# A small load of two rows of x per DMA engine, issued ahead of c, at the start of a DiT block

## The chip, the cores and the metric

The kernel runs on one core of one Trainium2 chip. The metric is the device time of one execution in microseconds (us). Executions quoted here: 3 to 11 of each kernel in one set of rounds; a span or a start time comes from the one profiled execution of that kernel. PE is the matmul engine, PEld its weight load, DVE the vector engine, ACT the scalar engine, POOL GpSimd; SPq and ACTq are the queues from which DMAs are issued.

## The reference, cut to what matters

```python
B, N, D = (2, 256, 1152)
mod = (_silu(c) @ w_mod).reshape(B, 6, 1, D)
shift_a, scale_a, gate_a, shift_m, scale_m, gate_m = [mod[:, i] for i in range(6)]
h = _layernorm(x, axis=-1) * (1 + scale_a) + shift_a
qkv = (h @ wqkv).reshape(B, N, 3, H, Dh)
# ... attention, output projection, second layernorm, two large matmuls with gelu
return x + gate_m * m
```

Only the first line of work matters here: the layernorm of x and the scale that comes from c. They must be done before the first large matmul can run.

## The kernel before

x is loaded as four tiles of 128 tokens, in the order 0, 1, 3, 2 (0 and 1 are batch 0). c goes out on the scalar queue at the same moment. Behind x come the weights; the first of them is w_scale_a, the columns of w_mod that make scale_a.

```python
    x_sb = act.tile([P, NT, D], BF16, name="x_sb", tag="x_sb")
    c_sb = act.tile([B * KD, P], BF16, name="c_sb")
    nc.scalar.dma_start(c_sb[:], c_v)
    for t in (0, 1, 3, 2):
        nc.sync.dma_start(x_sb[:, t, :], x_v[:, t // TPB, t % TPB, :])
    # ... constants, then the weights on the sync queue behind x
```

PE warms up on zeros, transposes c, and goes on warming up. ACT and DVE make `sT`, silu of c transposed:

```python
    warm(2, pwarm)
    nc.tensor.transpose(pc[:], c_sb[:], ident[0:B * KD, 0:B * KD])
    nc.scalar.activation(sig[:], pc[:], ACT.Exp, scale=-1.0)
    nc.vector.tensor_scalar_add(sig[:], sig[:], 1.0)
    nc.vector.reciprocal(sig[:], sig[:])
    nc.vector.tensor_tensor(sT..., pc..., sig..., op=ALU.mult)   # arguments cut
```

The layernorm statistics are divided: ACT takes tiles 0 and 2 (two passes each, into `sink`), DVE takes tiles 1 and 3.

## Time and profile before

| | before |
|---|---|
| time | 243.78 us median of 3 (243.64 to 244.18) |
| span of the profiled execution | 241.8 us |
| PE busy | 235.4 us, 97% |
| PE starts tile 2's transposes | 11.41 us |
| from there to the start of the last stage (at 168.34 us, in the chain of waits) | 156.93 us |

From the profile page of the kernel before: busy time by engine, the granted clock of PE in 40 slices (in tenths), and the chain of waits by engine.

```profile
PE 235.4 (97%) x1688; PEld 144.4 (60%) x1698; DVE 91.5 (38%) x193; ACT 59.9 (25%) x121; POOL 28.3 (12%) x47
...
PEclk9999999999999999999999999999999999999999
...
PE 94%; issue 2%; ACT 2%; POOL 1%; DVE 0%; POOLq 0%; DVEq 0%; ACTq 0%
```

The reader sees a kernel bound by PE from end to end. In this trace, a change at the start can only save or cost time where PE still waits, which is before 11.4 us. The next fence shows that stretch, from the timeline of the kernel before. The columns are start and length in us, engine, line, operation, what it writes and reads; in brackets, the engine's idle time just before and what ended it.

```profile
0.73 0.62 ACTq L84 DMA_DIRECT2D c_sb<-in_c_dram  x1
...
3.18 0.10 PEld L176 LDWEIGHTS <-c_sb 18*128 18x128 bf16 x1 [0.65 <-DMA c_sb<-in_c_dram]
...
3.30 4.29 PE L173 MATMUL pwarm<-zeros 128*128 128x256 f32 x14
3.41 0.19 ACT L178 ACTIVATE sig<-pc 128x18 f32<-128x18 bf16 x1 [0.74 <-PE pc L176]
...
3.66 1.25 ACT L206 ACTIVATE sink<-x_sb 128x1152 f32<-128x1152 bf16 x1
...
4.22 0.24 DVE L181 TENSOR_TENSOR sT<-pc,sig 128x18 bf16<-128x18 bf16 x1
...
4.76 1.48 DVE L193 BATCH_NORM_STATS2 stats<-x_sb 128x6 f32<-128x384 bf16 x3 [0.31 <-DMA x_sb<-in_x_dram]
...
6.63 0.23 POOL L342 TENSOR_SCALAR dm<-dm 128x1 f32<-128x1 f32 x1 [4.17 <-DVE dm L213]
...
6.90 0.29 ACT L335 ACTIVATE rstd<-dsq,dm 128x1 f32<-128x1 f32 x1 [0.51 <-POOL dm L342]
...
7.52 1.24 ACT L206 ACTIVATE sink<-x_sb 128x1152 f32<-128x1152 bf16 x1
...
11.41 0.28 PE L264 MATMUL pt<-ident,xn 128*128 128x128 bf16 x2 [0.29 <-DVE xn L233]
```

The tile view of x in the kernel before gives the time from issue to landing over the four tiles:

```profile
DMA to landing us min/median/max: 2.9/4.0/5.1
```

Asked for each load on its own, the same trace gives 2.9, 3.6, 4.5 and 5.1 us in order of issue. The issues start at about 0.73, 1.15, 1.6 and 2.1 us.

### The profile page before, as it was taken

The page shows a single profiled execution, that of the slowest core. Times are in us where ns is not written, and L with a number is a line of the kernel's source. Part 1 is how long each engine was busy: PE and PEld are TensorE (multiplying, and loading weights), DVE is VectorE, ACT ScalarE, POOL GpSimd, SP SyncE. Part 2 cuts the span into 40 slices and gives each one's busy share as a digit, 9 for nine tenths or more (in the row PEclk, how much of TensorE's full clock was granted, in tenths as well). Part 3 has the DMA queues.
Part 4 walks back from the last instruction along what each step waited for, and adds up shares of the span by engine and source line. Part 5 has one row for each costly group of instructions (what it writes and reads, how often), then busy time and mean ns, then how long its engine had stood idle before and what let it go on. Part 6 is the DMA issues. An engine that isn't in the chain of part 4 may idle for free.

```text
span 241.8 us, 3979 instructions
## 1 busy us (share of the span) xinstructions
PE 235.4 (97%) x1688; PEld 144.4 (60%) x1698; DVE 91.5 (38%) x193; ACT 59.9 (25%) x121; POOL 28.3 (12%) x47
## 2 busy tenths in 40 slices
PE   8799999999999999999999999999999999999994
PEld 5585444465567566888844444444556665566674
DVE  3742442319325678830002999960010000000001
ACT  6633322307215032671422333222000000000000
POOL 2300000002300324100000000001121111111111
PEclk9999999999999999999999999999999999999999
DMA  6999999997579999239999999999200000000000
GB/s 188 327 317 310 378 366 393 389 391 247 147 263 398 387 377 159 49 59 361 391 391 391 340 327 284 274 327 284 98 16 16 20 16 16 19 18 19 27 23 16
DMA packets 48781, 53.29 MB, mean 220 GB/s; under 512 B 9587, under 2 KB 36475, under 8 KB 48763
## 3 DMA queue, kind: packets, MB, share of 16 engines
q1 hardware_dynamic: 41312, 50.14, 62.5%
q10 hardware_dynamic: 6939, 1.71, 4.7%
q0 software_dynamic: 512, 1.19, 1.5%
q8 instruction: 13, 0.21, 0.4%
q14 instruction: 5, 0.04, 0.0%
HBM read 50.14 MB, written 1.19 MB: 212 GB/s over the span
## 4 chain that ended last, share of the span: by engine, by line
PE 94%; issue 2%; ACT 2%; POOL 1%; DVE 0%; POOLq 0%; DVEq 0%; ACTq 0%
PE pacc L799 29%; PE pacc L743 29%; PE pacc L690 7%; PE pacc L599 7%; PE pq L521 7%; PE pk L280 5%; PE pk L309 2%; PE pa L639 2%; PE ps_s L556 2%; PE pn L416 2%; ACT sink L206 1%; PE pt L264 1%; PE pm L247 1%; PE pg L498 0%; ACT rstd L335 0%
## 5 line engine op out<-in xcount | busy, mean ns | idle before, releaser
L743 PE MATMUL pacc<-hT,w_f 128*128 128x256 bf16 (+1 forms) x427 | 70.3, 325 | 0.3
L799 PE MATMUL pacc<-w_f,gT 128*128 128x384 bf16 (+2 forms) x468 | 70.5, 314 | 0.0
L799 PEld LDWEIGHTS <-gT 128*128 128x128 bf16 x468 | 44.4, 98 | 26.2
L743 PEld LDWEIGHTS <-w_f 128*128 128x128 bf16 x432 | 42.2, 98 | 27.6
L805 DVE TENSOR_TENSOR tmp<-pacc,gate 128x384 f32<-128x384 f32 (+2 forms) x13 | 6.9, 527 | 65.6 <-PE pacc L799 57.2
L775 ACT ACTIVATE gT<-pacc 128x512 bf16<-128x512 f32 x24 | 14.3, 597 | 32.6 <-PE pacc L743 32.6
L469 DVE SCALAR_TENSOR_TENSOR part<-w_gate_m,s,part 128x1152 f32<-128x1152 bf16 x16 | 21.4, 1414 | 0.0
L807 POOL TENSOR_TENSOR o_sb<-tmp,x 128x384 bf16<-128x384 f32 (+1 forms) x12 | 11.7, 973 | 54.0 <-DVE tmp L805 54.0
L690 PE MATMUL pacc<-w_o,big 128*128 128x384 bf16 x108 | 17.9, 326 | 0.0
L521 PE MATMUL pq<-hT,w_q 128*128 128x512 bf16 x79 | 17.7, 379 | 0.1
L599 PE MATMUL pacc<-w_v,hT 128*128 128x384 bf16 x108 | 17.7, 326 | 0.0
L599 PEld LDWEIGHTS <-hT 128*128 128x128 bf16 x108 | 10.5, 98 | 7.1 <-issue 0.3
L690 PEld LDWEIGHTS <-big 128*128 128x128 bf16 x108 | 10.4, 98 | 7.2 <-issue 0.4
L521 PEld LDWEIGHTS <-w_q 128*128 128x128 bf16 x81 | 7.9, 98 | 9.4
L280 PE MATMUL pk<-big,w_k 128*128 128x256 bf16 (+1 forms) x70 | 13.1, 324 | 0.1
L696 POOL TENSOR_TENSOR x<-tmp,x_sb 128x384 f32<-128x384 f32 x8 | 7.3, 914 | 27.4 <-DVE tmp L695 27.4
L467 DVE TENSOR_SCALAR part<-w_gate_m,s 128x1152 f32<-128x1152 bf16 x2 | 1.6, 818 | 22.3 <-DMA w_gate_m<-in_w_mod_dram 22.3
L491 POOL DMA_DIRECT2D gates_dram<-nat_v x2 | 1.1, 536 | 67.7 <-DVE nat_v L489 67.7
L280 PEld LDWEIGHTS <-w_k 128*128 128x128 bf16 x72 | 6.7, 97 | 3.7 <-issue 0.3
L764 ACT ACTIVATE gT<-pacc 128x512 bf16<-128x512 f32 x12 | 6.5, 598 | 8.9 <-PE pacc L743 8.9
L512 POOL DMA_DIRECT2D gates_dram<-nat x4 | 2.3, 584 | 49.3 <-DVE nat L509 48.7
L695 DVE TENSOR_TENSOR tmp<-pacc,gate 128x384 f32<-128x384 f32 x12 | 6.6, 549 | 3.1 <-PE pacc L690 3.1
(102 smaller groups left out, 164.2 us busy)
## 6 DMA issues: line engine op xcount, KB each, us to landing
w_f<-in_w_fc_dram SPq DMA_DIRECT2D x12, 864.0 KB, 14.9
w_f<-in_w_fc_dram SPq DMA_DIRECT2D x3, 1728.0 KB, 7.9
w_f<-in_w_fc_dram SPq DMA_DIRECT2D x2, 2592.0 KB, 17.2
w_gate_a<-in_w_mod_dram SPq DMA_DIRECT2D x3, 864.0 KB, 11.9
w_v<-in_wqkv_dram SPq DMA_DIRECT2D x3, 864.0 KB, 13.8
w_o<-in_wo_dram SPq DMA_DIRECT2D x3, 864.0 KB, 14.0
w_shift_m<-in_w_mod_dram SPq DMA_DIRECT2D x3, 864.0 KB, 6.6
w_scale_m<-in_w_mod_dram SPq DMA_DIRECT2D x3, 864.0 KB, 12.1
```

Of the source, the lines that this page charges most:

```text
L280: nc.tensor.matmul(pk[m][:, c0:c1], w_k[:, k, m * P:(m + 1) * P], hT0[:, k, c0:c1], start=(k == 0 and c0 == 0), stop=(k == KD - 1), skip_g ...
L469: nc.vector.scalar_tensor_tensor(part[:, b, :], wg[:, k, :], s32[:, k, b:b + 1], part[:, b, :], op0=ALU.mult, op1=ALU.add,)
L521: nc.tensor.matmul(pq[m][:], w_q[:, k, m * P:(m + 1) * P], hT[:, k, :], start=(k == 0), stop=(k == KD - 1), skip_group_check=True,)
L599: nc.tensor.matmul(pacc[:], hT[:, k, t * P:(t + 1) * P], w_v[:, k, pnl * PW:(pnl + 1) * PW], start=(k == 0), stop=(k == KD - 1),)
L690: nc.tensor.matmul(pacc[:], aT[:, k, t * P:(t + 1) * P], w_o[:, k, c0:c1], start=(k == 0), stop=(k == KD - 1),)
L695: nc.vector.tensor_tensor(tmp[:], pacc[:], gate_a[:, b, c0:c1], op=ALU.mult)
L696: (nc.gpsimd if pool_add else nc.vector).tensor_tensor(x1[:, t, c0:c1], tmp[:], x_sb[:, t, c0:c1], op=ALU.add)
L743: nc.tensor.matmul(dst, w_f1[m // KD][:, k, ml * P:(ml + 1) * P], hT[:, k, c0:c1], start=start, stop=(k == KD - 1), **kw,)
L775: nc.scalar.activation(gT[:, m, :], pacc[:], ACT.Gelu_apprx_tanh)
L799: nc.tensor.matmul(pacc[:], gT[:, kk, t * P:(t + 1) * P], w_f2[j][:, r, c0 - n * PW:c0 - n * PW + cw], start=(kk == 0), stop=(kk == KF - 1),)
L805: nc.vector.tensor_tensor(tmp[:], pacc[:], gate_m[:, b, c0:c0 + cw], op=ALU.mult)
L807: (nc.vector if last else nc.gpsimd).tensor_tensor(o_sb[:], tmp[:], x1[:, t, c0:c0 + cw], op=ALU.add)
```

## The change

The intent: in the trace of before, most packets of x (2304 bytes) took 93 ns, but some stood for 0.5 to 1.4 us while batch 1 was being read. A tiny load is put ahead, which reads 64 bytes of each of 32 rows of batch 1, meant as two rows for each of the 16 DMA engines, so that such waits are met early and overlapped. The loaded bytes are never used. That the waits belong to a first access, and that an early read takes them away, is supposition and not something the trace of before shows.

```diff
     c_sb = act.tile([B * KD, P], BF16, name="c_sb")
+    touch_x = act.tile([16, 2, 32], BF16, name="touch_x")
+    nc.scalar.dma_start(touch_x[:], x.rearrange("b (e r) d -> e b r d", e=16)[:, 1, 0:16:15, 0:32])
     nc.scalar.dma_start(c_sb[:], c_v)
```

## The prediction

> **What bounds the kernel now.** In the page of the kernel before, PE is busy 235.4 of 241.8 us (97%), the granted clock is 9 tenths or more throughout, and the chain of waits is 94% PE. From 11.41 us on PE hardly stops (gaps of 0.05 us), so earlier loads can gain only in the first 11.4 us. There the timeline shows a chain on ACT: c's DMA issue 0.73 to 1.35 us; PE transposes c at 3.18, having waited 0.65 for that DMA; the exponential of sig 3.41 to 3.60; then back to back the statistics of x tile 0 (from 3.66), their root, the statistics of tile 2 (7.52 to 10.24), its root, the DVE normalisation at 10.94, and tile 2's transposes on PE at 11.41, before which PE idled 0.29 us.
>
> **What the change is for.** The packets of x in the trace mostly took 93 ns, but those from batch 1 on (3.1 to 5 us) contain stalls of 515, 972, 811, 856, 552, 581 and 1439 ns, and DMA throughput dips from about 370 to about 230 GB/s in 3.75 to 5.6 us. The touch makes each DMA engine pay such first accesses early. I take that to work at least in part: the last batch 1 tile (issue 2.1, 5.1 us to landing, so 7.2) should land 0.5 to 1 us sooner, and the weights behind it too.
>
> **What that is worth.** Almost nothing. Tile 2 lands at 7.2, and ACT takes it up at 7.52 because its own chain ends then; tile 3 lands at 6.05 and DVE takes it up at 6.44 without waiting. The first piece of w_scale_a lands near 9.2 and its PE group starts at 9.26, but PE then waits at 11.41 for ACT's chain, not for weights.
>
> **What it costs.** One more issue on ACT ahead of c. c's took 0.62 us, x's on SP 0.38 to 0.43; I estimate 0.4 to 0.6 us for the touch. c goes out that much later, and PE was waiting for c. The 32 pieces of 64 bytes also go to the engines that carry c and x tile 0: the Trainium skill ("DMA: Bandwidth & Descriptors", section "Issuing engines are not separate DMA queues") says that all queues run on the same 16 engines and interleave. The trace agrees: five of c's 18 packets came at 2.5 us, 0.7 us after the others, amid stalled x packets. So touch stalls can delay c, or tile 0 (landing 3.63, just before its use), by some tenths more. I expect c's transpose at 3.8 us (3.5 to 4.6), the statistics of tile 0 at 4.3 rather than 3.66, and tile 2's transposes on PE at 12.0 rather than 11.41. The rest follows rigidly, since PE has no slack to give back: a loss of 0.6 us.
>
> **Predicted:** 244.4 us, range 243.5 to 245.3; faster by over 2%: 1%, within 2%: 98%, slower: 1%.
>
> **What would show it.** In the ACT timeline, sig and the first statistics 0.4 to 0.9 us later. Fewer or shorter long packets of x after 3.1 us, and batch 1's landings up to 1 us earlier. PE's idle time before tile 2's transposes about 0.9 us; from there every stage as long as before (lines 743 and 799 at about 70 us each).
>
> **What would make it wrong.** The ACT queue may hide the second issue: then the time is unchanged. In runs without a profile batch 1 may land later than in this trace, with ACT or DVE waiting for tiles 2 and 3: then the touch gains some tenths. Or the touches stall the engines by about 1 us each, before c and tile 0: then the loss is 1 to 2 us.

One count in it is off: in the trace of before four of c's 18 packets came late (2.49 to 2.54 us, the others at 1.71 to 1.80), not five.

## More of the kernel before

Every engine works in this program order:

```python
    warm(7, pwarm)
    act_stats(0)                 # ACT: dsum, dsq of tile 0
    for j in range(NPD):
        stats_piece(1, j)        # DVE: tile 1
    act_mean_eps(0)              # DVE: dm2 from dsum of tile 0; POOL: dm2 + eps
    act_root(0)                  # ACT: needs dm2
    # ... root of tile 1
    act_stats(2)                 # ACT: tile 2
    for j in range(NPD):
        stats_piece(3, j)        # DVE: tile 3
    # ...
    norm1(2, 0, CUT)             # DVE: normalise tile 2
    transpose_x([0, 1], [2], pt_c, 0)   # PE: tile 2, then the large matmuls
```

Note where `act_mean_eps(0)` stands: the small product that ACT's first root needs is queued on DVE behind the whole of tile 1.

## The result, and the profile after

The changed kernel took 243.49 us (median of 4, 243.47 to 243.59), the kernel before in the same rounds 243.71 us (median of 4, 243.63 to 244.18). The ratio is 0.999, with a 95% interval of 0.9975 to 1.0005. Ratios here are the mean time of one kernel's runs over the mean of the other's of the same rounds, so not quite the ratio of the medians quoted. The predicted loss of 0.6 us did not come; the measured median lies 0.01 us below the predicted range and 0.9 us below the predicted time.

The page of the changed kernel (busy time by engine, chain of waits by engine):

```profile
PE 236.3 (98%) x1688; PEld 144.9 (60%) x1698; DVE 91.3 (38%) x193; ACT 59.8 (25%) x121; POOL 28.3 (12%) x47
...
PE 94%; issue 2%; ACT 2%; POOL 1%; DVE 0%; POOLq 0%; DVEq 0%; ACTq 0%
```

PE is busy 0.9 us more in a span that is 0.1 us shorter, though it has the same matmuls to do; where that comes from is seen under experiment 3. The timeline of the changed kernel, with the lines that answer to those above:

```profile
0.73 0.41 ACTq L85 DMA_DIRECT2D touch_x<-in_x_dram  x1
...
1.17 0.59 ACTq L86 DMA_DIRECT2D c_sb<-in_c_dram  x1
...
3.60 0.10 PEld L178 LDWEIGHTS <-c_sb 18*128 18x128 bf16 x1 [1.07 <-DMA c_sb<-in_c_dram]
...
3.72 5.12 PE L175 MATMUL pwarm<-zeros 128*128 128x256 f32 x14
3.83 0.19 ACT L180 ACTIVATE sig<-pc 128x18 f32<-128x18 bf16 x1 [0.74 <-PE pc L178]
3.91 1.25 ACT L208 ACTIVATE sink<-x_sb 128x1152 f32<-128x1152 bf16 x1
...
4.63 0.24 DVE L183 TENSOR_TENSOR sT<-pc,sig 128x18 bf16<-128x18 bf16 x1
4.73 1.47 DVE L195 BATCH_NORM_STATS2 stats<-x_sb 128x6 f32<-128x384 bf16 x3
...
6.59 0.23 POOL L344 TENSOR_SCALAR dm<-dm 128x1 f32<-128x1 f32 x1 [4.13 <-DVE dm L215]
...
6.85 0.29 ACT L337 ACTIVATE rstd<-dsq,dm 128x1 f32<-128x1 f32 x1 [0.23 <-POOL dm L344]
...
7.48 1.24 ACT L208 ACTIVATE sink<-x_sb 128x1152 f32<-128x1152 bf16 x1
...
11.37 0.28 PE L266 MATMUL pt<-ident,xn 128*128 128x128 bf16 x2 [0.16 <-DVE xn L235]
```

c is late, as predicted: it is transposed 0.42 us later (3.60 against 3.18). The lateness then dies out. ACT starts tile 0 0.25 us later (3.91 against 3.66). DVE starts tile 1 at 4.73, now straight behind `sT` and without waiting for x, against 4.76 with a wait. That 0.42 us could vanish behind a displayed wait of 0.31 us is due to overlap: DVE began tile 1's statistics 0.10 us after the start of its `sT` instruction (4.63 to 4.73), before the recorded end of it. So in the kernel before DVE could have begun at 4.32, and its true room was about 0.44 us (an estimate from these two traces). That the lateness of 0.42 us just fits is luck of this landing. So POOL's step and ACT's root come at the same time as before (6.85 against 6.90), and what was lost on ACT is taken from its idle time there: 0.51 us before, 0.23 us now. From the root on everything is 0.04 us earlier, tile 2's transposes included (11.37 against 11.41). The last stage starts at 168.30 us, 156.93 us after those transposes, exactly as before: this part of the prediction held.

The tile view of x in the changed kernel:

```profile
DMA to landing us min/median/max: 2.7/3.6/4.7
```

The landings after issue are 2.7, 3.0, 4.1 and 4.7 us, each 0.2 to 0.6 us shorter than before, by these rounded figures. One pair of traces cannot tell whether that is the touch.

### The profile page after: what moved, and what is told of

Its sections match the earlier page's. It is cut to its first block, busy times and chain, and to the rows that moved or that the text cites. A ratio compares the mean times of both kernels' runs of the same rounds, so it can differ in the third digit from the quotient of the medians. Undisturbed runs are those within 1.5% of the kernel's fastest.

```text
span 241.7 us, 3980 instructions
## 1 busy us (share of the span) xinstructions
PE 236.3 (98%) x1688; PEld 144.9 (60%) x1698; DVE 91.3 (38%) x193; ACT 59.8 (25%) x121; POOL 28.3 (12%) x47
## 3 DMA queue, kind: packets, MB, share of 16 engines
q10 hardware_dynamic: 6987, 1.71, 5.2%
## 4 chain that ended last, share of the span: by engine, by line
PE 94%; issue 2%; ACT 2%; POOL 1%; DVE 0%; POOLq 0%; DVEq 0%; ACTq 0%
PE pacc L801 29%; PE pacc L745 29%; PE pacc L692 7%; PE pacc L601 7%; PE pq L523 7%; PE pk L282 5%; PE pk L311 2%; PE pa L641 2%; PE ps_s L558 2%; PE pn L418 2%; ACT sink L208 1%; PE pt L266 1%; PE pm L249 1%; PE pg L500 0%; ACT rstd L337 0%
## 5 line engine op out<-in xcount | busy, mean ns | idle before, releaser
L175 PE MATMUL pwarm<-zeros 128*128 128x256 f32 x18 | 7.2, 572 | 1.2 <-DVE eps_t L95 1.2
```

The costliest lines, as they stand in the source:

```text
L175: nc.tensor.matmul(dst[:, 0:T // 2], zeros32[:, 0:P], zeros32, start=True, stop=True)
```

## The experiments

The rival accounts were these. *Prediction's account*: the ACT chain from c binds, and lateness of c is lost from the first tenth on. *Theory D*: DVE binds, by the later of two events, `sT` done and tile 1 landed; lateness of c is free until the first passes the second, then lost one for one. Beside these stands the question whether the touch itself brings x earlier, and whether its rows matter. All 18 runs gave correct results.

| run | c | touch | this, us (median; range) | before, same rounds (median; range) | ratio (95%) |
|---|---|---|---|---|---|
| r1_before_again | on time | none | 243.87; 243.62 to 244.08 | 243.78; 243.18 to 244.30 | 1.0004 (0.9987 to 1.0021) |
| r2_after_again | late | batch 1 | 243.73; 243.49 to 243.76 | as above | 0.9996 (0.9982 to 1.0011) |
| r3_touch_c | late | c | 243.56; 243.51 to 243.62 | as above | 0.9993 (0.9979 to 1.0007) |
| r4_touch_behind_c | on time | batch 1 | 243.62; 243.32 to 243.96 | as above | 0.9995 (0.9979 to 1.0011) |
| r5_touch_batch0 | late | batch 0 | 243.83; 243.61 to 244.27 | 243.65; 243.25 to 244.60 | 1.0004 (0.9985 to 1.0023) |
| r9_two_touches | later still | batch 1 and c | 245.01; 244.78 to 245.50 | as above | 1.0053 (1.0033 to 1.0072) |
| r10_c_late_no_touch | late | none | 243.89; 243.61 to 244.08 | as above | 1.0004 (0.9985 to 1.0022) |
| r8_sig_late_touch_behind_c | on time | batch 1 | 243.65; 243.38 to 244.09 | as above | 0.9999 (0.9979 to 1.0020) |
| r6_sig_late | on time | none | 243.99; 243.53 to 244.31 | 243.79; 243.59 to 245.32 | 0.9999 (0.9976 to 1.0022) |
| r14_after_third | late | batch 1 | 243.72; 243.52 to 244.41 | as above | 0.9992 (0.9971 to 1.0014) |
| r13_gap_filled | late | batch 1 | 243.57; 243.51 to 243.61 | as above | 0.9983 (0.9959 to 1.0006) |
| r15_c_late_no_touch_gap_filled | late | none | 244.09; 243.88 to 244.38 | as above | 1.0004 (0.9982 to 1.0026) |
| r16_filled_touch_batch1 | late | batch 1 | 243.55; 243.48 to 243.84 | 243.68; 243.18 to 244.27 | 0.9992 (0.9977 to 1.0007) |
| r17_filled_touch_c | late | c | 243.53; 243.52 to 243.94 | as above | 0.9995 (0.9980 to 1.0011) |
| r18_filled_touch_batch0 | late | batch 0 | 243.83; 243.49 to 244.64 | as above | 1.0007 (0.9990 to 1.0025) |
| r19_filled_no_touch | late | none | 243.90; 243.64 to 244.19 | as above | 1.0008 (0.9993 to 1.0022) |
| r20_touch_from_gpsimd | on time | batch 1 | 243.50; 243.21 to 243.77 | 243.43; 243.16 to 244.55 | 0.9992 (0.9973 to 1.0010) |
| r21_gap_filled_again | late | batch 1 | 243.76; 243.60 to 244.34 | as above | 1.0007 (0.9989 to 1.0024) |

Runs that share a column "before" ran on the same chip. Only one of the 18 is clear of noise against before: r9. The kernel before alone ranges over a microsecond or more in every set of the table. That is the scale against which all the small differences below have to be read.

### 1. How much is lateness of c worth?

**The kernel before again** (r1, no edit but a blank line).

> The kernel before, unchanged (one blank line more). It measures how far a second trace and a second set of times differ from the first. Theory D (the start is bound by DVE: x tile 1 lands, DVE takes its statistics, and ACT's first root waits for what DVE computes behind them): tile 1 lands 4.6 to 4.8 us after the start, DVE starts its statistics at that moment, ACT idles about 0.5 us before its first root; time within 0.1 us of the kernel before. If instead the landing of tile 1 moves by 0.3 us or more from trace to trace, the earlier landing seen in the trace after the change can be chance, and what the change gained is not shown by one trace.

Two lines of its timeline:

```profile
5.02 1.48 DVE L194 BATCH_NORM_STATS2 stats<-x_sb 128x6 f32<-128x384 bf16 x3 [0.56 <-DMA x_sb<-in_x_dram]
...
7.15 0.30 ACT L336 ACTIVATE rstd<-dsq,dm 128x1 f32<-128x1 f32 x1 [0.76 <-POOL dm L343]
```

In this execution tile 1 landed 0.26 us later than in the first trace, and DVE, ACT's root and tile 2's transposes (11.69 against 11.41) came later by 0.25 to 0.28 us with it. Theory D's chain moved as one piece with the landing, while c was transposed at 3.19, as before. It also shows that the landing of tile 1 moves by some 0.3 us from one execution to the next, so that the first pair of traces proves nothing about the touch.

**c late, without a touch** (r10). c's issue waits for a DVE instruction that ends at 1.13 us:

```diff
-    nc.scalar.dma_start(c_sb[:], c_v)
-    nc.vector.memset(eps_t[:], LN_EPS)
+    eps_set = nc.vector.memset(eps_t[:], LN_EPS)
+    c_load = nc.scalar.dma_start(c_sb[:], c_v)
+    tc.add_manual_dep(c_load.ins, eps_set.ins.name, WAIT_FOR, reason="c late")
```

> No touch: c alone is issued about 0.45 us later, because its issue waits for DVE's memset of eps at 1.1 us. It tells the lateness of c from the small reads. If what brings tile 1 earlier in all four kernels with a small load (4.1 to 4.5 us against 4.7 to 5.0 in two traces of before) is that c's packets no longer run ahead of the first packets of x, tile 1 lands at 4.1 to 4.5 here too, and the time is 243.5 to 243.7. If it is the small load, tile 1 lands at 4.7 to 5.0, DVE starts there, and the time and its spread are those of before (median about 243.8, spread about 0.7 us). The prediction's theory says 244.2 to 244.4 in either case.

The timeline of that kernel:

```profile
4.84 1.47 DVE L194 BATCH_NORM_STATS2 stats<-x_sb 128x6 f32<-128x384 bf16 x3
...
6.96 0.29 ACT L336 ACTIVATE rstd<-dsq,dm 128x1 f32<-128x1 f32 x1 [0.22 <-POOL dm L343]
...
11.60 0.27 PE L265 MATMUL pt<-ident,xn 128*128 128x128 bf16 x2
```

c was transposed at 3.71 us, 0.53 us late. DVE started tile 1 straight behind `sT` at 4.84 without a wait for x, and ACT's idle time before the root was 0.22 us instead of 0.51. The time was 1.0004 of before, so about +0.1 us, with an interval that holds zero. The prediction's account asked for +0.4 to +0.6. In r15 and r19, two more kernels with c late and no touch, the ratio was 1.0004 and 1.0008. The cost of this lateness is therefore about 0.1 to 0.2 us, an estimate from three ratios of which none is clear of 1; each interval alone reaches up to a loss of 0.5 to 0.6 us, so these times do not exclude the prediction's term by themselves. The trace does, for its execution: the root moved by 0.06 us. The other traces agree on the size: DVE started on tile 1 at 4.43 to 5.02, on average 4.68, in the four traces with c on time and `sT` in its place (before, r1, r4, r20), and at 4.73 to 4.98, on average 4.79, in the thirteen with c late by 0.4 to 0.7 us. In r10 tile 2's transposes came 0.19 us late (11.60) although the root was nearly on time, and PE had not idled before them: here PE itself was behind, as section 3 tells.

**A second small load ahead of c** (r9):

```diff
     nc.scalar.dma_start(touch_x[:], x.rearrange(...)[:, 1, 0:16:15, 0:32])
+    touch_y = act.tile([16, 2, 32], BF16, name="touch_y")
+    nc.scalar.dma_start(touch_y[:], c.rearrange("b (e r) -> e b r", e=16)[:, :, 0:32])
     nc.scalar.dma_start(c_sb[:], c_v)
```

> The changed kernel with a second small load (of c) on the scalar queue, so that c goes out about 0.84 us later than in the kernel before, double the changed kernel's delay. Theory D (free up to the landing of tile 1, then time lost one for one): sT is done about 0.85 us later than before, DVE starts the statistics of tile 1 at 5.1 to 5.2 us (4.73 to 4.78 in the changed kernel), ACT's first root moves from 6.85 to about 7.2 to 7.3 us, tile 2's transposes on PE move from about 11.4 to 11.7 to 11.9, and the time is 0.2 to 0.4 us above the changed kernel. The prediction's theory has the loss grow with the delay from zero on, so 0.8 us above before, about 244.5. If the first weights bind PE instead, the time stays at 243.5 to 243.7.

The timeline of that kernel:

```profile
4.50 0.10 PEld L180 LDWEIGHTS <-c_sb 18*128 18x128 bf16 x1 [1.98 <-DMA c_sb<-in_c_dram]
...
5.64 1.47 DVE L197 BATCH_NORM_STATS2 stats<-x_sb 128x6 f32<-128x384 bf16 x3
...
7.76 0.29 ACT L339 ACTIVATE rstd<-dsq,dm 128x1 f32<-128x1 f32 x1 [0.23 <-POOL dm L346]
...
12.28 0.28 PE L268 MATMUL pt<-ident,xn 128*128 128x128 bf16 x2 [0.30 <-DVE xn L237]
```

c came later than intended: it was transposed at 4.51, which is 1.33 us behind before (expected 0.84). DVE started tile 1 at 5.64, 0.88 us late, and the root (7.76) and tile 2's transposes (12.28) were late by 0.86 and 0.87 us. The time rose by 0.53%, about 1.3 us, and this is clear of noise. So lateness does cost, once it is past the landing of tile 1; the first 0.4 to 0.5 us had been free. The rise is more than the 0.87 us that the chain shows. The trace accounts for the rest: behind the landing of the last store SyncE (the engine that issues the sync queue) goes through semaphore instructions of 0.06 us each, two in before and eight in r9, and the program ends 1.33 us after that landing instead of 0.97. These 0.36 us go with the additional load and not with the lateness of c; without them about 0.9 us are left for the chain. The time alone, a rise of 0.8 to 1.8 us by its interval, could not tell theory D (0.9) from the prediction's account (1.33, the whole lateness); the steps in the trace do.

**sT out of DVE's way** (r6): in the kernel before, the three DVE instructions that make `sT` go behind `act_mean_eps(0)`.

> The kernel before with DVE's three instructions that make sT moved behind the statistics of tile 1. Theory D says that in the kernel before DVE waits for the landing of tile 1, not for c: so taking the c work out of DVE's way changes nothing, DVE starts at the landing (4.4 to 5.0 us), and the time and its spread stay those of before (within 0.15 us). If DVE were held by the chain from c, its start would move 0.3 us earlier and the time would fall by 0.2 to 0.3.

The timeline of that kernel:

```profile
4.37 1.48 DVE L187 BATCH_NORM_STATS2 stats<-x_sb 128x6 f32<-128x384 bf16 x3 [3.24 <-DMA x_sb<-in_x_dram]
...
6.62 0.24 DVE L346 TENSOR_TENSOR sT<-pc,sig 128x18 bf16<-128x18 bf16 x1
```

DVE now waited for x alone and started at the landing, 4.37 us in this execution. The time was 0.9999 of before. That fits theory D but proves little: ACT's root came at 6.50, 0.40 us sooner than in the first trace of before, yet tile 2's transposes came at 11.28, only 0.13 us sooner, with PE busy right up to them. PE's own queue would have hidden most of a gain.

### 2. Does the touch bring x earlier, and by its rows?

**The changed kernel again, and the touch of c in its place** (r2 and r3; r2 has no edit but a blank line):

```diff
-    nc.scalar.dma_start(touch_x[:], x.rearrange("b (e r) d -> e b r d", e=16)[:, 1, 0:16:15, 0:32])
+    nc.scalar.dma_start(touch_x[:], c.rearrange("b (e r) -> e b r", e=16)[:, :, 0:32])
```

> The changed kernel, unchanged (one blank line more). If the touch really brings x tile 1 earlier, tile 1 lands at 4.0 to 4.4 us again (4.15 in the first trace, 4.73 before) and the time is 0.1 to 0.3 us below the kernel before. If that landing was chance, it is anywhere from 4.1 to 4.8 us and the time is within 0.1 us of before.

> The touch with the same shape, at the same place, but reading 32 pieces of c instead of x: c is late as in the changed kernel (its issue ends about 0.4 us later), and nothing of x is touched. The prediction's theory (ACT's chain binds, so c late is time lost): time 0.3 to 0.6 us above before. Theory D: c late by 0.4 us moves DVE's first vector work to an end of about 4.85 to 4.95 us, and x tile 1 lands at about 4.7 us as before, so DVE loses 0.1 to 0.2 us at most and the time is 0 to 0.2 us above before. If the reading of x is not what brings tile 1 earlier, tile 1 lands at about 4.2 us here too and the time equals that of the changed kernel.

In r2 tile 1 landed at about 4.55 us (3.4 after issue, against 3.0 in the first trace), outside the range expected of a touch that works, and tile 2 at about 7.7. In r3, where nothing of x is touched, tiles 1 and 2 landed at about 4.25 and 6.25, and no other trace has tile 2 so early. DVE started tile 1 at 4.77 and 4.78, straight behind `sT`, in both. The prediction's account failed here too: r3 is not above before (0.9993, and at most 1.0007, which is 0.17 us).

**Touch of batch 0** (r5: the index `1` in the touch becomes `0`).

> The touch at the same place and of the same size, reading two rows of batch 0 per engine (rows that the first loads of x read at the same moment) instead of batch 1. If touching the rows of batch 1 were what helps, tiles 3 and 2 would land as in the kernel before (6.0 to 6.3 and 7.2 to 7.5 us) and later than in the changed kernel (5.4 to 5.7 and 6.8 to 7.7 in two traces). If the rows do not matter, which the touch of c suggests (5.4 and 6.3 us), nothing sets this kernel apart: tile 1 lands at 4.1 to 4.5 us, DVE starts its statistics at 4.73 to 4.78 behind sT, time 243.5 to 243.7 with a spread below 0.3 us.

c was later (transposed at 3.85), tile 1 landed near 4.8, and the time was 243.61 to 244.27: the spread expected below 0.3 us was 0.66. This expectation missed. Tiles 3 and 2 landed at 6.08 and 7.44, where the text expected them if the rows matter; but in r18, below, with the same touch, they landed at 5.62 and 6.52, and only r3 had tile 2 earlier.

**Four kernels on one chip that differ in what the small load reads** (r16 to r19). All have c equally late (transposed at 3.61 or 3.62 us) and the gap on PE filled, as told in the next section. They followed on a first pair of this kind, r13 and r15, told there.

> Gap filled, touch of batch 1, as in the run of that kind before. Rows matter: 243.5 to 243.65 with a spread below 0.2 us, tile 2 landing by 7.5 us so that ACT takes it up at 7.5 to 7.6 without waiting. Chance: anywhere from 243.5 to 244.4.

> Gap filled, touch of c. Rows matter: like the kernel without a touch, 243.6 to 244.4 with a spread of 0.4 us or more, tile 2 landing after 7.5 us in part of the executions. Any small load ahead helps: 243.5 to 243.65, as the first touch of c.

> Gap filled, touch of batch 0. Rows matter: like the kernel without a touch, 243.6 to 244.4, and perhaps c later still (3.85 us in the first such run). Any small load ahead helps: 243.5 to 243.65.

> Gap filled, c late, no touch, as in the run of that kind before: 243.8 to 244.4, spread 0.4 us or more, with tile 2 landing at 7.5 to 8 us and ACT waiting for it. If it comes out at 243.5 to 243.65 this time, the difference of the first pair was the luck of that pair.

The means were 243.59 (batch 1), 243.62 (c), 243.91 (batch 0) and 243.92 (none). So two of the touches are 0.3 us below no touch, and one is not. With r13 and r15 (243.57 and 244.08, ranges that do not overlap) this makes two pairs in favour of the touch of batch 1, by 0.33 and 0.51 us. But the touch of c does as well, which "the rows of batch 1" does not explain, and the traces show no order: tile 2 was taken up by ACT at 7.59, 7.49, 7.49 and 7.56. (A trace is one execution: that of r16 was the slowest of its group, those of r18 and r19 the fastest of theirs.) The times thus suggest a gain of the touch and the landings do not show its mechanism.

The packets speak against the supposed mechanism. In the thirteen traces with a 64-byte touch on the scalar queue every packet of the touch took 8 to 11 ns, so none of them stood in place of a packet of x. And the packets of x that started after 3.05 us and took over 400 ns were 6 to 13 in the six traces with c late and the touch of batch 1 alone, and 5 to 11 in the six without a touch, the longest 0.75 to 1.78 us and 0.57 to 2.06 us. What the traces do show is a small saving that has nothing to do with x: behind the landing of the last store the program ends 0.90 to 0.91 us later in all twelve traces with one small load on the scalar queue, and 0.96 to 0.97 in the seven without one (r20 among them). SyncE has one semaphore instruction less to go through there in the changed kernel than in before. So about 0.06 us of each difference comes from the end of the program.

**The touch from GpSimd, and the filled gap a third time** (r20 and r21). In r20 the touch is issued by `nc.gpsimd`, so c is on time; r21 is r16 again.

```diff
+    nc.gpsimd.dma_start(touch_x[:], x.rearrange("b (e r) d -> e b r d", e=16)[:, 1, 0:16:15, 0:32])
     nc.scalar.dma_start(c_sb[:], c_v)
```

> The touch of batch 1's rows is issued from the GpSimd queue instead of the scalar queue, so c goes out first on its own queue, at 0.73 us, as in the kernel before. Two separate terms: c is transposed at about 3.2 us, DVE starts on tile 1 when it lands (4.4 to 4.8 us), tile 2 lands by 7.5 us in nearly all executions, and the time is 243.2 to 243.5 with a spread below 0.4 us. If the touch comes too late from this queue or delays GpSimd's own start-up work (the identity that c's transpose needs), c's transpose moves and the time is that of before or above.

> Gap filled, touch of batch 1, once more: 243.5 to 243.65 for nearly all executions (10 of 11 so far), about 0.1 to 0.2 us below before. If this third group spreads like before (0.7 us or more), the narrow spread of the first two was luck.

r21 missed: 243.60 to 244.34, a mean of 243.82 where the two earlier groups had 243.57 and 243.59, and 1.0007 of before. Its trace shows one more place where loads set the time, in PE's waits after 11 us:

```profile
20.04 0.60 PE L251 MATMUL pm<-sT,w_scale_a 128*128 128x2 bf16 x18 [0.17 <-DMA w_scale_a<-in_w_mod_dram]
```

There a late piece of w_scale_a held PE at 20 us. In the kernel before, the same group started at 19.57 without a wait. Another 0.3 us was lost at the start of the first of the two large matmuls with gelu (98.43 us, against 97.62 in before), for a reason that was not followed up. r20 had c on time (3.19), tile 1 taken up at 4.50 and tile 2 at 7.54, after 0.2 us of waiting for it; its time was 0.9992 of before, with a range (243.21 to 243.77) wider than expected. The steps of the chain held, and no gain in time is shown.

**The touch behind c** (r4 and r8). In r4 the touch follows c on the scalar queue; r8 also moves `sT` as r6 does.

> The touch of x issued behind c on the scalar queue instead of ahead of it: c is on time (transposed at about 3.2 us, sT done at about 4.45 us). Theory D: if x tile 1 still lands at about 4.2 us, DVE starts its statistics at about 4.45 us in place of 4.75, ACT's first root comes 0.3 us sooner, and the time is 0.2 to 0.4 us below before and 0.1 to 0.3 below the changed kernel, unless the first weights (landing at 9.2 to 9.4 us) hold PE up. The prediction's theory: c on time restores before exactly, so the time equals before within 0.1 us. If the touch comes too late in this place, tile 1 lands at about 4.7 us and the time equals before too; the landing tells these two apart.

> Touch behind c, and DVE's three instructions that make sT moved behind the statistics of tile 1 and the small product that ACT's root waits for. Theory D: DVE starts on tile 1 the moment it lands (4.2 to 4.5 us), ACT's first root comes when ACT's own statistics end (6.4 us) with no or little idle time, 0.4 to 0.5 us sooner than before; tile 2's statistics then wait for its landing (6.8 to 7.3), so tile 2's transposes on PE come at 11.1 to 11.3 us, and the time is 0.1 to 0.3 us below the changed kernel if the first weights (PE's first group of scale at 9.3 to 9.8 us) do not bind, else equal to it.

From the timeline of r4:

```profile
4.43 1.48 DVE L195 BATCH_NORM_STATS2 stats<-x_sb 128x6 f32<-128x384 bf16 x3
...
6.56 0.30 ACT L337 ACTIVATE rstd<-dsq,dm 128x1 f32<-128x1 f32 x1 [0.16 <-POOL dm L344]
...
11.27 0.28 PE L266 MATMUL pt<-ident,xn 128*128 128x128 bf16 x2
```

Here theory D's steps can be followed in the traces: c on time (3.18), DVE on tile 1 at 4.43 and 4.42, ACT's root at 6.56 in both (6.90 before), tile 2's transposes at 11.27 and 11.28 (11.41 before), spans of 241.6 us. PE idled at most 0.08 us before those transposes. In r4 its first group of scale had waited 0.33 us for w_scale_a and started at 9.33; in r8 it started at 9.59 without such a wait, behind first transposes of x that came only at 9.15, because DVE had made `sT` in between. So 0.34 us gained at the root leaves 0.13 us at the transposes: the next limit, PE's own queue, is that close. The times, 0.9995 and 0.9999 of before, do not resolve it. No kernel is shown to beat both; the lowest single executions (243.16 and 243.18) are of the kernel before.

### 3. A side effect of late c: PE warms up later

The traces showed a second thing that moved with c. While PE waits for c it idles (0.35 us in the changed kernel), and its warm-up matmuls then stay slow for longer. The Trainium skill, "TensorE: Matmul & The Clock Gate", section "What's actually happening", says that the PE clock is halved until a free-running window of 3413 ns has been busy. The trace agrees in the durations: the warm-up matmuls start 0.43 us apart at first and 0.22 us apart later. The granted clock that the trace records does not show it; it reads 1.00 in this stretch in both kernels. In the six kernels with c on time and the seven with the gap filled, the step came between 4.7 and 7.7 us; in the seven with c late and the gap open, between 7.1 and 8.7. The first matmul starts at 1.18 us, and PE resumes after the gap at 3.7 to 4.6, so this is 3.5 to 6.5 us after the one and 3.1 to 4.9 us after the other: about one to two windows, if the wait starts afresh each time (a reading; 3.1 us is a little short of one). That is most of why PE was 0.9 us busier after the change: the same fourteen passes took 5.12 us instead of 4.29. In r2 the last of them ended so late that it, and no longer DVE, held the first transposes of x (from the timeline of r2):

```profile
3.77 5.81 PE L176 MATMUL pwarm<-zeros 128*128 128x256 f32 x14
...
9.41 0.39 PE L267 MATMUL pt<-ident,xn 128*128 128x128 bf16 x4
```

**The gap filled** (r13), beside the changed kernel a third time (r14, blank lines only) and the same without a touch (r15, which has r10's edit and this one):

```diff
     warm(2, pwarm)
+    nc.tensor.matmul(pwarm[:], zeros[:, 0:P], zeros[:], start=True, stop=True)
     nc.tensor.transpose(pc[:], c_sb[:], ident[0:B * KD, 0:B * KD])
```

> The changed kernel a third time, beside the next two kernels on the same chip. c is transposed at about 3.6 us after PE idled 0.35 us or more; by the traces so far PE's warm-up matmuls then go from 0.43 to 0.22 us each not before 7.1 us and the last of them ends at 8.8 to 9.6 us, where it holds up the first transposes in about half of the executions. DVE starts tile 1 at 4.73 to 4.78 us. Time 243.5 to 243.75.

> The changed kernel with one more warm-up matmul (0.43 us, its result is never read) in front of c's transpose, so that PE does not idle while c is late. If the gap is what delays PE's faster rate, the matmuls speed up between 4.6 and 8 us instead of 7.1 to 8.7, their last one ends before 8.8 us, and PE's first transposes start when DVE delivers (8.8). Then the time is 0 to 0.15 us below the changed kernel's of the same chip. If the gap has no part in it, nothing moves.

> c late by the same 0.45 us and the gap filled as in the run beside it, but no touch: so this and the run with the filled gap differ only in the touch. If the touch of batch 1's rows brings x earlier, tiles 1, 3 and 2 land 0.3 to 0.6 us later here than there, and the time is 0.1 to 0.3 us higher. If the touch does nothing, the landings overlap (tile 1 at 4.1 to 4.8 us, tile 2 at 6.5 to 7.7) and the times agree within 0.1 us.

From the timeline of r13:

```profile
3.85 4.38 PE L175 MATMUL pwarm<-zeros 128*128 128x256 f32 x14
...
8.91 0.40 PE L267 MATMUL pt<-ident,xn 128*128 128x128 bf16 x4 [0.68 <-DVE xn L236]
```

The fourteen warm-up passes took 4.38 us, against 5.19 in r14, and the first transposes again waited for DVE. One pair does not settle it: in r15, also with the gap filled, they took 5.06 us. All traces together do: the step came after 7.1 us in all seven with the gap open, and in only three of the thirteen without a gap (r8, r15, r19). So the gap delays the warm-up, though the step varies by 1.6 us among the former and by 3 us among the latter. This is also the way by which late c can still reach tile 2's transposes: in r2, r3 and r10, where the passes took 5.8 us, these came at 11.53 to 11.61 (11.41 before) with no idle time of PE before them. The price of the gap in time stays within noise: r13 had a mean of 243.57 and r14 one of 243.79, but r14 ranged from 243.52 to 244.41, and its own trace had the first transposes at 8.83 and tile 2's at 11.42, as before the change.

In r15 a third arrival shows, that of tile 2. From its timeline, ACT's statistics of tile 2:

```profile
7.96 1.25 ACT L208 ACTIVATE sink<-x_sb 128x1152 f32<-128x1152 bf16 x1 [0.31 <-DMA x_sb<-in_x_dram]
...
9.95 0.60 PE L249 MATMUL pm<-sT,w_scale_a 128*128 128x2 bf16 x18 [0.58 <-DMA w_scale_a<-in_w_mod_dram]
...
11.87 0.28 PE L266 MATMUL pt<-ident,xn 128*128 128x128 bf16 x2
```

Tile 2 landed 5.8 us after its issue, and ACT waited 0.31 us for it; tile 2's transposes came at 11.87. Not for tile 2 alone: in the same execution, the slowest of its group, PE waited 0.58 us for the first piece of w_scale_a at 9.95, and before 11.87 it stood idle for 0.07 us only. This fourth arrival held PE by 0.27 to 0.58 us in six of the twenty traces (r4, r15, r16, r19, r20, r21), with a touch and without. The prediction had read from the one trace of before that tile 2 lands 0.3 us ahead of need and called its landing worth almost nothing. It varies by more than that: 4.2 to 5.8 us from issue over all the traces.

## Why the prediction was wrong

- **Held: c goes out later.** By 0.41 us of issue (estimated 0.4 to 0.6) and 0.42 us at PE (3.60 us; predicted 3.8, range 3.5 to 4.6).
- **Failed: "PE was waiting for c", hence "a loss of 0.6 us".** The chain on ACT was read as "back to back" from c to the statistics of tile 2. It is not: the line of ACT's first root says 0.51 us idle, released by POOL, which follows DVE's work on tile 1, which waited for x to land. The prediction used that trace and did not follow this line. With late c the root came at 6.85 us against 6.90 (changed kernel). The term c late, predicted at +0.6 us, measures +0.1 to +0.2 us by r10, r15 and r19, none clear of zero. That lateness is paid beyond the free stretch is shown by r9: 1.33 us late at PE, 0.88 us late at DVE.
- **Not settled: the touch is worth "almost nothing".** Against kernels with c equally late and no touch, the touch of batch 1 was 0.51 and 0.33 us faster in two pairs on two chips, which would outweigh the 0.1 to 0.2 us of late c and fit the measured 0.999. The third group (r21) was not fast, and a touch of c was. So that batch 1's rows cause a gain is not shown, and about 0.06 us of any gain comes from the end of the program. The reasoning behind "almost nothing" was weak in any case: it took one trace's margins of 0.3 us as fixed, where landings move by more than that between executions (r1, r15, r21).
- **Not settled: batch 1 lands up to 1 us earlier.** It did by 0.4 us in the first pair. Tile 2's time from issue was 4.6 to 5.6 us in six traces with a late c and the touch of batch 1 alone, and 4.7 to 5.8 in six traces without a touch: these overlap. "Fewer or shorter long packets of x after 3.1 us", which the prediction named as a sign, were not found either (section 2).
- **Held: from tile 2's transposes on, the rest is rigid.** 156.93 us to the last stage in the traces of before, after, r1 and r9. PE is busy there nearly without a break. Four other traces (r10, r15, r16, r21) took 0.15 to 0.75 us more there; the largest is r21, of which 0.4 us were lost by 20 us, where a weight came late.
- **Failed: PE's idle time before tile 2's transposes "about 0.9 us".** It was 0.16 us.
- **Listed and true in part:** "In runs without a profile batch 1 may land later than in this trace". r15 shows such an execution, with ACT waiting for tile 2, but without a touch; with one, r20's ACT waited 0.2 us too.

## What to carry to other kernels

Before charging a delay to a chain, follow each link's idle time and its releaser: a chain that looks back to back on one engine may hold a wait for another engine, and a delay is free up to the size of that wait. Where two arrivals race, such as two loads, take the spread of each from several executions; a margin of 0.3 us read from one trace is no margin when landings move by as much. A change worth a tenth of a per cent needs a control that differs in one thing on the same chip, repeated; here a clean-looking pair did not repeat.

## What the Trainium skill lacked or had wrong

- "TensorE: Matmul & The Clock Gate", section "What's actually happening": no length is given for an idle gap during the warm-up that puts off the faster rate. Here 0.35 us on PE was enough: the faster rate came at 7.1 to 8.7 us instead of 4.7 to 7.7.
- "DMA: Bandwidth & Descriptors", section "Issuing engines are not separate DMA queues", calls the sequencer's issue time "usually small relative to the DMA itself". It gives no figure. For the touch of 2 KB it was 0.41 us of ACT's queue here, of 2.5 us from issue to landing; for c's 4.5 KB it was 0.59 to 0.62 us.
- "DMA: Bandwidth & Descriptors", section "Latency and other measured facts", gives the HBM access latency as 0.2 us on average and 2 us at high load. Single packets of x stood for up to 2.06 us (r15) among packets of 93 ns, which does not contradict it. No page says what makes one packet stand that long, or whether an earlier small read of the same region shortens it; these runs show no fewer such packets with the touch.
- No page gives the spread of a load's landing between executions. Tile 2 of x took 4.2 to 5.8 us from issue over the traces here.
